# A mixture of experts handing over to a second network: tap weights, row transposes, last copies and half of a weight split put in another order

## The chip, the core and the metric

One core of a Trainium2 chip runs the whole program. TensorE (PE) multiplies and transposes into PSUM, ScalarE (ACT) and VectorE (DVE) copy, cast and compute, GpSimd (POOL) issues gathers and scatters, SyncE (SP) issues the other transfers. Each engine works through a queue of its own. The metric is the device time of the program in microseconds (us); lower is better.

## The reference, cut to what matters

A windowed attention (not touched) makes `x` of 4 x 544 tokens by 512. Then come two networks:

```python
for b in range(B):                       # mixture of experts, one expert e per token
    for s in range(S):
        h = np.maximum(x[b, s] @ w1[e], 0.0)
        out[b, s] = p[e] * (h @ w2[e])

h = np.maximum(x @ w_in, 0.0)            # second network, on out
for k in range(K):                       # K = 3 taps along the tokens
    conv_out += conv_w[k][None, None, :] * hp[:, k:k + S, :]
gate = 1.0 / (1.0 + np.exp(-conv_out))
return (h * gate @ w_out).astype(np.float32)
```

A token has 512 features, an expert 1024 hidden ones, and so has the second network.

## The kernel before, in words

Every float32 product is made as three TensorE products of a high and a low part: `split_k` (L1043) makes the parts of a weight block (a cast `h`, by default on ScalarE, and a subtraction `l` on VectorE; blocks 1, 3, 5 and 7 of the second network's output weights have the cast on VectorE too).

**Mixture of experts.** Tokens are sorted by expert into slots of 128 rows. A slot is gathered, turned (`turn_x`), multiplied by `w1` (`layer1`), turned (`turn_h`), multiplied by `w2` (`layer2`), copied from PSUM to `ys` by ScalarE and scattered to `y_dram` by GpSimd. `step` runs slots 2 to 19 as a pipeline. While they run, the second network's weights are loaded and converted. `last(21)` handles slots 20 and 21 together: `p` is 20 and `s` is 21. Each part of a slot stands in a run-time branch (`either`): a slot of at most 32 rows takes the short path `few_l1`, `few_turn`, `few_l2`, which uses unsplit weights; then the second network's weights can be split early, under a branch on the same flag (`r`, L1229 to L1232 for the input weights).

**The passage.** In `last` the order, written out by hand, is: slot 21's rows turned; the input weights split; a sigmoid on a scratch column (L1233, it loads the function table that the second network uses); slot 19's second layer (`layer2(p - 1)`), its copy and scatter; the load of the second network's first rows from `y_dram` (`load0`, five transfers); slot 21's `few_l1`; slot 20's turn; slot 21's `few_turn`; the taps' transpose (`conv_w`, L1184 and L1185); a flag that says whether late tokens touch those rows (`late_flag`, L962 to L964); slot 20's second layer; the five row parts scaled by the gate (`scale0`, VectorE); parts 0 and 1 turned and split (`xt0`: four TensorE transposes, a ScalarE cast, a VectorE subtraction); slot 21's `few_l2` with its four copies (L1422) and the scatter; parts 2 to 4 turned. `run` then reads the flag (L1196, L1197), does the rest only if it is set, and splits the eight blocks of the output weights (`split_out`).

**Second network.** It runs over 32 units (batch `b`, feature block `f`). A unit is 24 products (L1589), a relu (L1613), three taps (L1606, L1608), a sigmoid (L1623), a gating product (L1624) and a split (L1636, L1637). In units 0 to 3 ScalarE also scales the next batch's rows (L1545), which SyncE loads from `y_dram` (L1539) once the last scatter has landed. In program order the first L1545 stands between unit 0's taps and unit 1's relu.

Of the kernel before, what the change touches and what calls it, by code (L numbers as in the profile page):

```python
# [8 lines left out]
F32 = mybir.dt.float32  # L9
# [3 lines left out]
AF = mybir.ActivationFunctionType  # L13
# [4 lines left out]
P = 128  # L18
B, H, SL, SG, DH = 4, 8, 512, 32, 64
S = SL + SG  # L20
DM = H * DH
E, FF = 8, 1024
NKC = DM // P
NFC = FF // P
# [27 lines left out]
def build_masks(nc, pool, masks):  # L52
# [16 lines left out]
    for g in range(2):  # L69
        e = nc.gpsimd if g else nc.vector  # L70
        for t in range(3):
            rows = slice(64 * g, 64 * g + 32)
            for slot, o in enumerate(win_order(t)):
                if o in (0, 2):
                    e.tensor_copy(masks[rows, t, 32 * slot:32 * slot + 32], (lo, hi)[o // 2][rows])
            yield
        rows = slice(64 * g + 32, 64 * g + 64)
        for t in range(2):
            for slot, o in enumerate(win_order(2)):
                dst = masks[rows, t, 32 * slot:32 * slot + 32]  # L80
                if o == 2 * t:
                    e.memset(dst, BIG)
                elif o in (0, 2):
                    e.tensor_copy(dst, (lo, hi)[o // 2][rows])
        yield
# [900 lines left out]
NTS = P // TS  # L986
# [8 lines left out]
FILL = {1: 1, 3: 1, 6: 3, 7: 1, 8: 3, 9: 1, 10: 1, 11: 1, 12: 2, 13: 3, 15: 5, 16: 8}  # L995
HALF = 5
K_LAST = 2
N_GLOB = 6
N_GS = 4
N_Y = 24  # L1000
# [8 lines left out]
def conv64(nc, raw, out, m, lim):  # L1009
    hi, lo = raw[:, :, 1], raw[:, :, 0]  # L1010
    v, a, n = nc.vector, out.bitcast(I32), m.shape[0]
    nc.scalar.activation(m, hi.bitcast(F32), AF.Abs)
    nc.scalar.activation(m.bitcast(I32), m, AF.Sign, bias=lim[0:n], scale=-1.0)
    v.tensor_scalar(a, hi, 3, 0x3FFFFFFF, ALU.logical_shift_left, ALU.bitwise_and)
    v.scalar_tensor_tensor(a, hi, -2 ** 30, a, ALU.bitwise_and, ALU.bitwise_or)
    v.scalar_tensor_tensor(a, lo, 29, a, ALU.logical_shift_right, ALU.bitwise_or)
    v.tensor_scalar(lo, lo, 28, 1, ALU.logical_shift_right, ALU.bitwise_and)
    v.tensor_tensor(a, a, m.bitcast(I32), ALU.bitwise_and)  # L1018
    nc.gpsimd.tensor_tensor(a, a, lo, ALU.add)  # L1019
# [33 lines left out]
class Moe:  # L1053
# [133 lines left out]
    def run(self, cw6, cwr, cw, f2):  # L1187
        nc, W, tc = self.nc, self.W, self.tc
        n = NSLOT - 3
        self.f2 = f2  # L1190
        for s in range(NA, n - 2):
            self.step(s)
            if s == NA + 17:
                conv64(nc, cw6, cwr, f2.x_in[4][0:3 * NFC, 0:P], self.lim)
        self.last(n - 1, cwr, cw)
        r = nc.values_load(self.rt.esi[0:1, 4, 1:2], min_val=0, max_val=P + 1)  # L1196
        with tc.If(r != 0):  # L1197
            r = nc.values_load(self.rt.esi[0:1, 4, 0:1], min_val=0, max_val=NB)
            with tc.If(r > n - NA):
                for s in range(n, NSLOT):  # L1200
                    self.slot(s)
            f2.load0()
            for i in range(5):
                f2.scale0(i, self.ps)
                f2.xt0(i, self.ps)
        self.split_out()

    def last(self, s, cwr, cw):
        nc, W, f2, p = self.nc, self.W, self.f2, s - 1
        self.small(s)  # L1210
        self.layer1(p)
        self.fetch(p, 1)
        self.turn_x(s)
        self.resplit(s, 1)
        x, xs, hp = self.xt.pop(s), self.xs.pop(s), self.h_tile()
        hs = self.tp.tile([P, FF], F32, tag="hs", name="hs")
        ht = tuple(self.tp.tile([P, NFC, P], F32R, tag="g" + q, name="g" + q) for q in "hl")
        y = self.ys[s % 2]

        def split(a, b):  # L1220
            for k in range(a, b):
                W.split_k(1, W.f, k, nc.vector)

        def resplit(a, b):
            with self.tc.If(self.chg[s] != 0):
                for k in range(a, b):
                    W.split_k(2, W.s, k, nc.vector)

        r = nc.values_load(self.rt.esi[0:1, 5, s:s + 1], min_val=0, max_val=1,  # L1229
                           engines=[mybir.EngineType.Activation, mybir.EngineType.DVE])  # L1230
        with self.tc.If(r != 0):
            split(0, NKC)  # L1232
        nc.scalar.activation(self.sig, self.sig, AF.Sigmoid)  # L1233
        self.layer2(p - 1)
        self.fetch(p - 1, 2)
        f2.load0()
        with self.tc.If(self.sm[s] != 0):
            self.few_l1(xs, hp, hs)
        self.turn_h(p)
        self.resplit(p, 2)  # L1240
        t = [self.ps.tile([P, 4, P], F32, tag="tr", name="hlp") for _ in range(2)]

        def full1():
            for k in range(K_LAST):
                self.l1_mm(x, W.t[1], hp, k, range(2))
            split(0, K_LAST)

        tq = self.px.tile([P, 4, P], F32, tag="tr", name="hlq")
        self.either(s, lambda: self.few_turn(hs, tq), full1)
        self.conv_w(cwr, cw)  # L1250
        self.rt.late_flag(s + 1, self.px.tile([P, 4, P], F32, tag="tr", name="lf")[0:1, 0, 0:1])
        self.layer2(p)
        self.fetch(p, 2)
        for i in range(5):
            f2.scale0(i, self.ps)
        resplit(0, 4)
        for i in range(2):
            f2.xt0(i, self.px)
        yp = self.y_tile()

        def full2():
            for k in range(K_LAST, NKC - 1):
                self.l1_mm(x, W.t[1], hp, k, range(2))
            for c in range(2):
                self.l1_mm(x, W.t[1], hp, NKC - 1, (c,))
                self.relu_c(hp, hs, c)
            for a in (0, 4):
                for k in range(4):
                    nc.tensor.transpose(t[a // 4][:, k, :], hs[:, P * (a + k):P * (a + k) + P], self.ident)
                nc.scalar.copy(ht[0][:, a:a + 4], t[a // 4])  # L1270
            for a in (0, 4):
                self.lo_t(ht, a, t[a // 4])
            split(K_LAST, NKC)

        self.either(s, lambda: self.few_l2(hs, yp, y), full2)
        resplit(4, NFC)
        with self.tc.If(self.sm[s] == 0):
            for k in range(NFC):
                self.l2_mm(ht, W.t[2], yp, k)
            nc.scalar.copy(y, yp)  # L1280
        self.scatter(s, y)
        for i in range(2, 5):
            f2.xt0(i, self.ps if i == 4 else self.px)

    def split_out(self):
        nc, W = self.nc, self.W
        for k in range(NFC):
            W.split_k(2, W.f, k, nc.gpsimd if k in POOL_F else nc.vector, nc.vector if k in DVE_F else None)

    def slot(self, s):  # L1290
        nc, W = self.nc, self.W
        xs = self.gather(s)
        e = self.reg(nc.sync, 0, s, E - 1)
        for n, w in ((1, self.w1), (2, self.w2)):
            W.load(n, w[bass.ds(e, 1)])
        hs = self.tp.tile([P, FF], F32, tag="hs", name="hs")
        self.turn(xs, NKC)
        hp, yp = self.h_tile(), self.y_tile()
        for k in range(NKC):
            for c in range(2):  # L1300
                nc.tensor.matmul(hp[c], xs[:, P * k:P * k + P], W.s[1][:, k, 512 * c:512 * c + 512],
                                 start=k == 0, stop=k == NKC - 1)
        for c in range(2):
            self.relu_c(hp, hs, c)
        self.turn(hs, NFC)
        for k in range(NFC):
            nc.tensor.matmul(yp, hs[:, P * k:P * k + P], W.s[2][:, k, :], start=k == 0, stop=k == NFC - 1)
        self.out(s, yp)
# [104 lines left out]
    def few_l2(self, hs, yp, y):  # L1413
        n, w = FF // NTS // P, DM // NTS
        for k in range(NFC):
            j, a = divmod(k, n)
            o = P * (n + a) + TS * j
            for i in range(NTS):
                self.nc.tensor.matmul(yp[TS * i:TS * i + TS, 0:w], hs[:, o:o + TS], self.W.s[2][:, k, w * i:w * i + w],
                                      start=k == 0, stop=k == NFC - 1)  # L1420
        for i in range(NTS):
            self.nc.scalar.copy(y[P - TS:P, w * i:w * i + w], yp[TS * i:TS * i + TS, 0:w])  # L1422

# [68 lines left out]
class Ffn2:  # L1492
# [191 lines left out]
    def run(self):  # L1684
# [4 lines left out]
        for n in range(N):  # L1689
            if n < N:  # L1690
# [11 lines left out]
                if n == N_GS:  # L1702
                    x2["g"] = self.scaled(xs.pop("g"), GT)
                if n == N_GLOB:
                    self.glob(x2.pop("g"))
                if b + 1 < B and f == N_GLOB:
                    self.put_glob(b + 1, x[b + 1])
# [197 lines left out]
```

## Time and profile before

| what | value |
|---|---|
| median of 3 runs | 611.85 us (610.93 to 612.66) |
| the profiled execution's own time | 610.53 us |
| its span in the trace | 608.6 us |
| TensorE busy | 570.2 us, 94% |
| VectorE, ScalarE, GpSimd busy | 395.0, 331.4, 171.7 us |

The span is the time in the trace from the first instruction to the last; the 1.9 us between it and the own time lie outside it. Busy shares are over the whole program, and the passage is about 25 us of it (from 380 to 405 us), so the change is read from there.

### The profile page before, as it was taken

To read this page: it belongs to the slowest core of one execution; us is meant where nothing else is said; L and a number is where in the kernel's file an instruction comes from. 1 tells how busy PE (TensorE), PEld (TensorE's weight loads), DVE (VectorE), ACT (ScalarE), POOL (GpSimd) and SP (SyncE) were. 2 spreads that over 40 slices of the span, in tenths; PEclk is the share of its full clock that TensorE was granted. 3 is DMA by queue.
4 is the path that set the end of the run, shared out by engine and by line. 5 is a ranking of instruction groups with operands and counts; after the bars stand their busy time and mean duration, and the time that the engine had idled before them with its cause. 6 is when DMAs were issued, how large, how long until landed. Compare 5 with 4: busy or idle time off the path is not lost. (4 is left out here: it accounts for less than half of the span.)

```text
span 608.6 us, 16465 instructions
## 1 busy us (share of the span) xinstructions
PE 570.2 (94%) x6108; PEld 477.5 (78%) x6108; DVE 395.0 (65%) x821; ACT 331.4 (54%) x657; POOL 171.7 (28%) x226
## 2 busy tenths in 40 slices
PE   8789889879888999999999999889899999999997
PEld 7567667666666888887777788679898998998986
DVE  7877676865983857786487884457963574473330
ACT  5764555556324746865566774447762554463441
POOL 7655740025022332243142330010411403300100
PEclk9998999989899999999999999889999999999999
DMA  9989949656327964597366684321110210000001
GB/s 238 209 196 249 244 114 200 188 194 214 136 71 257 339 203 153 197 355 251 96 246 227 257 298 134 119 82 43 53 36 36 69 36 18 36 5 30 36 36 52
DMA packets 60644, 90.58 MB, mean 149 GB/s; under 512 B 25726, under 2 KB 34198, under 8 KB 60504
## 3 DMA queue, kind: packets, MB, share of 16 engines
q1 hardware_dynamic: 57016, 78.93, 42.5%
q0 software_dynamic: 3520, 10.23, 4.8%
q8 instruction: 65, 1.06, 0.8%
q14 instruction: 43, 0.35, 0.2%
HBM read 125.87 MB, written 15.79 MB: 233 GB/s over the span
## 5 line engine op out<-in xcount | busy, mean ns | idle before, releaser
L1608 DVE SCALAR_TENSOR_TENSOR fc<-f_hp,cw,fc 128x544 f32<-128x544 f32 (+2 forms) x66 | 51.4, 779 | 70.1 <-ACT fc L1606 68.7
L1046 DVE TENSOR_TENSOR wl<-ws,wh 128x512 fp32r<-128x512 f32 (+1 forms) x80 | 65.1, 874 | 16.5 <-ACT wh L1045 13.3
L1045 ACT CAST wh<-ws 128x512 fp32r<-128x512 f32 (+1 forms) x84 | 57.9, 772 | 2.8 <-DMA ws<-in_moe_w_dram 1.8
L1126 PE MATMUL yp<-wh,gh 128*128 128x512 f32 x136 | 55.9, 411 | 1.1 <-ACTq L1340 0.9
L1126 PE MATMUL yp<-wl,gh 128*128 128x512 f32 x136 | 54.8, 403 | 0.4 <-DVEq L1340 0.4
L1666 PE MATMUL f<-wh,fh 128*128 128x512 f32 (+1 forms) x144 | 54.8, 380 | 0.0
L1666 PE MATMUL f<-wh,fl 128*128 128x512 f32 (+1 forms) x144 | 54.4, 378 | 0.0
L1666 PE MATMUL f<-wl,fh 128*128 128x512 f32 (+1 forms) x144 | 54.4, 378 | 0.0
L1126 PE MATMUL yp<-wh,gl 128*128 128x512 f32 x136 | 54.4, 400 | 0.0
L278 ACT ACTIVATE pr<-sp,nm 128x128 f32<-128x128 f32 x128 | 36.6, 376 | 25.0 <-DVE nm L275 25.0
L1083 POOL DMA_INDIRECT y_dram<-ys,sidx x22 | 24.3, 1102 | 90.2 <-ACT ys L1447 30.2
L1110 PE MATMUL hp<-wl,xh 128*128 128x512 f32 x136 | 43.9, 394 | 2.1 <-DVEq L1340 1.1
L1110 PE MATMUL hp<-wh,xh 128*128 128x512 f32 x136 | 45.3, 405 | 0.4 <-PE hlp L1433 0.2
L1071 POOL DMA_INDIRECT xs<-x_dram,gidx x22 | 25.6, 1163 | 70.2 <-ACT pr L278 34.0
L1110 PE MATMUL hp<-wh,xl 128*128 128x512 f32 x136 | 43.6, 392 | 0.0
L1318 ACT ACTIVATE hs<-hp 128x512 f32<-128x512 f32 x34 | 18.7, 596 | 43.1 <-PE hp L1110 42.2
L1613 ACT ACTIVATE f_hp<-f 128x544 f32<-128x544 f32 x31 | 19.4, 624 | 34.7 <-PE f L1589 34.6
L1019 POOL TENSOR_TENSOR wf<-wf,fx 128x512 int32<-128x512 int32 x16 | 20.9, 1308 | 60.0 <-DVE wf L1018 54.7
L1675 ACT COPY fy<-f 128x512 f32<-128x512 f32 (+1 forms) x18 | 10.1, 564 | 46.6 <-PE f L1666 46.6
L1126 PEld LDWEIGHTS yp<-wh,gh 128*128 128x128 f32 x136 | 26.3, 193 | 8.4 <-issue 2.3
L1110 PEld LDWEIGHTS hp<-wl,xh 128*128 128x128 f32 x136 | 25.1, 188 | 9.0 <-DVEq L1340 2.1
L1666 PEld LDWEIGHTS f<-wh,fl 128*128 128x128 f32 x144 | 27.1, 188 | 5.1
(384 smaller groups left out, 1514.2 us busy)
## 6 DMA issues: line engine op xcount, KB each, us to landing
ws<-in_moe_w_dram SPq DMA_DIRECT2D x42, 2048.0 KB
fx<-y_dram SPq DMA_DIRECT2D x17, 256.0 KB
raw<-in_k_l_dram SPq DMA_DIRECT2D x16, 256.0 KB
x_dram<-x SPq DMA_DIRECT2D x16, 256.0 KB
fx<-in_moe_w_in_dram SPq DMA_DIRECT2D x8, 512.0 KB
fx<-in_moe_w_out_dram SPq DMA_DIRECT2D x8, 512.0 KB
out_dram<-fy SPq DMA_DIRECT2D x16, 256.0 KB
VA<-in_v_l_dram SPq DMA_DIRECT2D x20, 192.0 KB
```

Source lines behind the costliest of these rows:

```text
L278: nc.scalar.activation(pr[:, hp, :], sp[:, hp, :], AF.Exp, bias=nm[:, hp:hp + 1], scale=-1.0)
L1019: nc.gpsimd.tensor_tensor(a, a, lo, ALU.add)
L1045: (cp.tensor_copy if cp else self.nc.scalar.copy)(h, src[n][:, k, :])
L1046: eng.tensor_tensor(l, src[n][:, k, :], h.bitcast(F32), ALU.subtract)
L1071: self.nc.gpsimd.indirect_dma_start(out=xs, out_offset=None, in_=self.x_dram[0:n, :], in_offset=bass.IndirectOffsetOnAxis(ap=self.rt.gidx[ ...
L1083: self.nc.gpsimd.indirect_dma_start(out=self.y_dram[:, :], out_offset=bass.IndirectOffsetOnAxis(ap=self.rt.sidx[:, s:s + 1], axis=0), in_= ...
L1110: self.nc.tensor.matmul(hp[c], a[:, k, :], b[:, 512 * c:512 * c + 512], start=k == 0 and m == 0, stop=k == NKC - 1 and m == 2)
L1126: self.nc.tensor.matmul(yp, a[:, k, :], b, start=k == 0 and m == 0, stop=k == NFC - 1 and m == 2)
L1318: self.nc.scalar.activation(hs[:, 512 * c:512 * c + 512], hp[c], AF.Relu)
L1608: nc.vector.scalar_tensor_tensor(c[:, a:b], hp[:, a + t:b + t], self.cw[:, t, f:f + 1], c[:, a:b], ALU.mult, ALU.add)
L1613: self.nc.scalar.activation(hp[:, 1:S + 1].rearrange("p (a c) -> p a c", a=2), p[:, :, 0:272], AF.Relu)
L1666: self.nc.tensor.matmul(yp[:, cs], x[:, c], w[:, cs], start=f == 0 and n == 0, stop=f == NFC - 1 and n == 2)
```

## The change

The taps' transpose moves ahead of the input weights' split, the late flag ahead of `few_l1`, and the table load behind `few_turn`. All five row parts are turned ahead of `few_l2`; slot 21's copies and scatter (`out_last`, `few_y`) move behind the branch on the flag. If slot 21 is short, blocks 0 to 3 of the output weights are split right behind `layer2(p)` in the program, blocks 4 to 7 where all eight were.

```diff
+K_OUT = 4
...
-        self.last(n - 1, cwr, cw)
+        yp = self.last(n - 1, cwr, cw)
         r = nc.values_load(self.rt.esi[0:1, 4, 1:2], min_val=0, max_val=P + 1)
         with tc.If(r != 0):
+            self.out_last(n - 1, yp)
...
-        self.split_out()
+        self.out_last(n - 1, yp)
+        with tc.If(self.few_last != 0) as c:
+            self.split_out(range(K_OUT, NFC))
+        with c.Else():
+            self.split_out()
...
-        r = nc.values_load(self.rt.esi[0:1, 5, s:s + 1], min_val=0, max_val=1,
-                           engines=[mybir.EngineType.Activation, mybir.EngineType.DVE])
+        r = self.few_last = nc.values_load(self.rt.esi[0:1, 5, s:s + 1], min_val=0, max_val=1,
+                                           engines=[mybir.EngineType.Activation, mybir.EngineType.DVE])
+        self.conv_w(cwr, cw)
         with self.tc.If(r != 0):
             split(0, NKC)
-        nc.scalar.activation(self.sig, self.sig, AF.Sigmoid)
         self.layer2(p - 1)
         self.fetch(p - 1, 2)
         f2.load0()
+        self.rt.late_flag(s + 1, self.px.tile([P, 4, P], F32, tag="tr", name="lf")[0:1, 0, 0:1])
         with self.tc.If(self.sm[s] != 0):
             self.few_l1(xs, hp, hs)
...
         self.either(s, lambda: self.few_turn(hs, tq), full1)
-        self.conv_w(cwr, cw)
-        self.rt.late_flag(s + 1, self.px.tile([P, 4, P], F32, tag="tr", name="lf")[0:1, 0, 0:1])
+        nc.scalar.activation(self.sig, self.sig, AF.Sigmoid)
         self.layer2(p)
         self.fetch(p, 2)
+        with self.tc.If(r != 0):
+            self.split_out(range(K_OUT))
         for i in range(5):
             f2.scale0(i, self.ps)
         resplit(0, 4)
-        for i in range(2):
-            f2.xt0(i, self.px)
+        for i in range(5):
+            f2.xt0(i, self.ps if i == 4 else self.px)
         yp = self.y_tile()
...
-        self.either(s, lambda: self.few_l2(hs, yp, y), full2)
+        self.either(s, lambda: self.few_l2(hs, yp, None), full2)
         resplit(4, NFC)
         with self.tc.If(self.sm[s] == 0):
             for k in range(NFC):
                 self.l2_mm(ht, W.t[2], yp, k)
-            nc.scalar.copy(y, yp)
+        return yp
+
+    def out_last(self, s, yp):
+        y = self.ys[s % 2]
+        self.either(s, lambda: self.few_y(yp, y), lambda: self.nc.scalar.copy(y, yp))
         self.scatter(s, y)
-        for i in range(2, 5):
-            f2.xt0(i, self.ps if i == 4 else self.px)
...
-    def split_out(self):
+    def split_out(self, ks=range(NFC)):
         nc, W = self.nc, self.W
-        for k in range(NFC):
+        for k in ks:
             W.split_k(2, W.f, k, nc.gpsimd if k in POOL_F else nc.vector, nc.vector if k in DVE_F else None)
...
-        hp, yp = self.h_tile(), self.y_tile()
+        hp, yp = self.h_tile(), self.px.tile([P, DM], F32, tag="tr", name="yp")
...
+        if y is not None:
+            self.few_y(yp, y)
+
+    def few_y(self, yp, y):
+        w = DM // NTS
         for i in range(NTS):
             self.nc.scalar.copy(y[P - TS:P, w * i:w * i + w], yp[TS * i:TS * i + TS, 0:w])
```

## Rows read from the trace of the kernel before

**Rows 1.** The page's first part: busy time of each engine.

```profile
PE 570.2 (94%) x6108; PEld 477.5 (78%) x6108; DVE 395.0 (65%) x821; ACT 331.4 (54%) x657; POOL 171.7 (28%) x226
```

**Rows 2.** The chain that ended last, in order of time: start, us, what.

```profile
435.33 0.30 POOL fxl L1573
435.68 6.15 PE f L1589 x46
```

**Rows 3.** Windows of 1 us: busy time by engine, granted clock, DMA share, GB/s.

```profile
389.00:390.00 1.00, 0.00 (x0) 0.00 (x0) 0.62 (x2) 0.37 (x1) 0.00 (x0) 1.00 0.69 262
...
392.00:393.00 1.00, 1.00 (x4) 0.81 (x3) 0.00 (x0) 0.00 (x0) 0.00 (x0) 0.50 0.54 139
```

**Rows 4.** Timeline ahead of slot 20's second layer: start, us, engine, line, operation.

```profile
381.51 3.90 ACT L1045 CAST wh<-wf 128x1024 fp32r<-128x1024 f32 x4 [1.16 <-DMA y_dram<-ys,sidx]
385.43 1.28 ACT L1233 ACT_TABLE_LOAD   x1
...
388.33 1.29 DVE L1103 TENSOR_TENSOR gl<-hlp,gh 128x512 fp32r<-128x512 f32 x2 [1.10 <-ACT gh L1434]
...
390.14 0.18 DVE L1185 COPY cw<-cwp 128x24 f32<-128x24 f32 x1 [0.53 <-DVEq L1349]
...
390.38 0.16 PE L962 MATMUL lf<-c_ones,late 128*1 128x1 bf16 x1 [1.88 <-DVE esi L963]
...
391.10 0.40 PE L1126 MATMUL yp<-wl,gh 128*128 128x512 f32 x1
...
391.56 0.56 PE L1126 MATMUL yp<-wh,gh 128*128 128x512 f32 x1
...
394.91 0.46 PE L1126 MATMUL yp<-wh,gl 128*128 128x512 f32 x1
```

**Rows 5.** Timeline from slot 20's second layer to slot 21's copies.

```profile
394.05 0.47 DVE L1513 TENSOR_SCALAR fx<-fx,gate 32x512 f32<-32x512 f32 x1 [3.32 <-DMA fx<-y_dram]
...
397.12 0.49 DVE L1513 TENSOR_SCALAR fx<-fx,gate 128x512 f32<-128x512 f32 x1 [0.53 <-DMA fx<-y_dram]
...
397.74 0.39 PE L1126 MATMUL yp<-wh,gl 128*128 128x512 f32 x1
...
398.22 0.59 ACT L1447 COPY ys<-yp 128x512 f32<-128x512 f32 x1 [8.82 <-PE yp L1126]
...
399.01 2.29 PE L1419 MATMUL yp<-ws,hs 128*32 128x128 f32 x64
...
399.21 0.29 DVE L1523 TENSOR_TENSOR f_x0l<-f_tr,f_x0h 128x128 fp32r<-128x128 f32 x1 [1.60 <-ACT f_x0h L1522]
399.73 0.69 DVE L1523 TENSOR_TENSOR f_x0l<-f_tr,f_x0h 128x512 fp32r<-128x512 f32 x1 [0.23 <-ACT f_x0h L1522]
...
401.44 1.50 PE L1520 MATMUL f_tr<-ident,fx 128*128 128x128 f32 x12
401.46 1.10 ACT L1422 COPY ys<-yp 32x128 f32<-32x128 f32 x4 [1.76 <-PEq L1277]
```

**Rows 6.** Timeline of the output weights' split and the second network's first products.

```profile
404.75 2.18 ACT L1045 CAST wh<-wf 128x512 fp32r<-128x512 f32 x4 [0.28 <-ACTq L1197]
...
405.53 0.59 PE L1589 MATMUL f<-f_x0l,wh 128*128 128x272 f32 x1 [0.56 <-DVEq L1197]
...
405.78 0.69 DVE L1046 TENSOR_TENSOR wl<-wf,wh 128x512 fp32r<-128x512 f32 x1 [0.36 <-DVEq L1197]
...
408.51 1.29 DVE L1046 TENSOR_TENSOR wl<-wf,wh 128x512 fp32r<-128x512 f32 x2
```

**Rows 7.** Timeline of SyncE and ScalarE in the second network's first units.

```profile
406.02 25.21 SPq L1539 DMA_DIRECT2D fx<-y_dram  x8
...
413.35 0.72 ACT L1545 ACTIVATE fx<-fx,gate 128x512 f32<-128x512 f32 x1 [1.81 <-DMA fx<-y_dram]
413.98 0.61 ACT L1613 ACTIVATE f_hp<-f 128x544 f32<-128x544 f32 x1
...
417.87 0.75 ACT L1606 ACTIVATE fc<-f_hp,cw 128x544 f32<-128x544 f32 x1 [0.84 <-DVE fg L1624]
```

More of the change, by code (lines that the diff above doesn't have):

```diff
@@ L1217, in last @@
         ht = tuple(self.tp.tile([P, NFC, P], F32R, tag="g" + q, name="g" + q) for q in "hl")
-        y = self.ys[s % 2]
         def split(a, b):
```

## The prediction, as it was put on record

> **What bounds the kernel now.** I read the busy shares first, then the chain that ended last, then the timeline of the passage engine by engine, because a share over 608.6 us says nothing about 25 of them. TensorE is busy 94% of the span [rows 1], so a delay that TensorE meets is paid in full unless the stretch behind it has slack. The chain shows where slack ends: at 435.68 us unit 8's first products follow at once on GpSimd's copy of 435.33, and from there to the end the chain is mostly TensorE [rows 2]. What matters is what sets 435.68. In units 1 to 7 it is ScalarE, fed by VectorE. At 413.35 ScalarE takes up the first row scaling after waiting 1.81 us for its transfer; unit 1's relu comes right behind at 413.98, and the next gap is a wait for VectorE, 0.84 us before 417.87 [rows 7]. So the path runs: slot 21's last copy of ys, its scatter, the row load, the first L1545, seven units on ScalarE and VectorE, unit 8. The last copy ends at 401.46 + 1.10 = 402.56 [rows 5], and L1545 starts 10.8 us later [rows 7]. I therefore ask one question: when does the last copy end after the change?
>
> All offsets below count from E, the end of slot 20's second layer, 397.74 + 0.39 = 398.13 [rows 5]. The last copy now ends at E + 4.43.
>
> **Up to E: what the moved tap turn, flag and table load give.** TensorE stands idle for 1.88 us before the flag's product at 390.38, which comes just after VectorE's taps copy of 390.14 to 390.32; the second product of slot 20's layer starts at 391.10 [rows 4], and the window from 389 shows no TensorE work [rows 3]. Both small products move to places where VectorE has long answered or nothing behind them needs the answer, and they cost TensorE about the same there. The new limit is VectorE: gl is done at 388.33 + 1.29 = 389.62, and VectorE reaches its next instruction 0.52 us later [rows 4]. I put the second product at 390.2, a gain of 0.9 us. The bounds are 0 (it waits as now) and 1.7 (it follows the turn without waiting, at 389.4). The idle time had a second price: eight products from 391.56 to 394.91 took 3.35 us where the pitch just before was 0.46 / 2 = 0.23 us [rows 4], with a granted clock of 0.50, the lower level, in that stretch [rows 3]. At the higher level they take 1.84, so 1.5 us come back if the remaining gaps leave the clock alone; 0 if not. I take both: 2.4 us, between 0 and 3.2.
>
> The table load, 1.28 us at 385.43 [rows 4], moves behind `few_turn`, where ScalarE next waits 8.82 us for slot 20's products [rows 5]. That wait hides it; uncovered it would cost its 1.28 us. It frees slot 19's copy and scatter by about as much, so the five first loads come earlier too, but they already land before E (the scalings run from 394.05 to 397.12 [rows 5]). They take nothing off the path.
>
> **From E on: the split ahead of the row scalings.** Slot 21 is short: the four early casts of the input weights ran at 381.51 [rows 4] and `few_l2` at 399.01 [rows 5]. So the new branch is taken. In the program, block 0's cast on ScalarE stands behind the copy of slot 20's ys, and that copy waits for slot 20's last product. VectorE's first new instruction is the subtraction that needs this cast, and the five scalings, now done by 397.61 under cover of the products [rows 5], stand behind it. So the blocks are not split beside slot 20's layer but behind it, and they take the scalings with them onto the path. In order:
>
> The copy of ys: starts 0.09 after E and takes 0.59, to 0.68 [rows 5]. Block 0's cast: 2.18 / 4 = 0.55 [rows 6], to about 1.25. VectorE's part of blocks 0 to 3: today the same six instructions run from 405.78 to 408.51 + 0.65 = 409.16 [rows 6], so 3.4, to 4.65. Five scalings: 0.47 + 4 x 0.49 = 2.4 [rows 5], to 7.1. Two branches that VectorE passes, at 0.36 each by the gap before 405.78 [rows 6], to 7.8. Low parts of rows 0 and 1: 0.29 + 0.69 [rows 5], to 8.8. These must finish first because all five parts are now turned ahead of `few_l2` and parts 0 to 3 share two PSUM buffers: part 3's turn waits for part 1's subtraction. Turns of parts 3 and 4: 8 of the 12 transposes that took 1.50 [rows 5], so 1.0, to 9.8. `few_l2`: 2.29 and 0.1 for its branch, to 12.2. Then 0.16 and the four copies, 1.10 [rows 5], to 13.45. Overlapped starts on VectorE could shave 0.45 off, so 13.0 is the lower end.
>
> TensorE is empty for about 5.5 us behind E and then does scattered transposes. The trace has the lower clock after 1.88 us of idling [rows 3, 4], so I expect it here. At the lower level the two turns and `few_l2` could take up to twice their 3.3 us; the surcharge lies between 0 and 3.3. I take 1.0, because part of the transposes runs while TensorE waits for VectorE anyway. That makes E + 14.45 against E + 4.43: 10.0 us later.
>
> What the smaller edits cost: the output weights' second half, split under a further branch, is shorter than what stood there (VectorE's eight blocks ran behind 405.78 [rows 6]), and with the load later still it is done before the first L1545, which hides it. The extra PSUM buffer use in `slot` belongs to slots that run only if the flag is set; the flag was not set here, so it costs nothing.
>
> **The sum.** 10.0 - 2.4 = 7.6 us later for the last copy, so for the scatter, the load and the first L1545, and the units behind it have no slack to give back. The profiled execution took 610.53 us (span 608.6 and 1.9 outside), so it would become 618.1. The shown median is 611.85, 1.3 above it; on that scale the forecast is 619.4. Ends: 13.0 - 4.43 - 3.2 = 5.4 and 13.45 + 3.3 - 4.43 = 12.3, so 617.2 to 624.2.
>
> One rule speaks about the link in the middle. The first load is issued at 406.02 and the second of the five is waited for until 413.35 [rows 7], 7.3 us. The Trainium skill ("DMA: Bandwidth & Descriptors", section on the anatomy of one DMA) gives about 2.0 us plus bytes / 436e3 for a transfer, in its fit for GpSimd's path; that is an estimate of 2.6 us for 256 KB. By it L1545 would be ready 4.7 us sooner and TensorE would set the units' pace, which is the second case below; by the row, the sum above stands.
>
> **The rivals.**
>
> *TensorE sets the pace, not the row load.* Then the shift is that of the stream of products, which now runs from 405.53, E + 7.4 [rows 6]. It would follow `few_l2` and a branch: 12.2 + 1.0 + 0.36 = 13.55. So 6.2 - 2.4 = 3.8 later, 615.6; with the best front gain and no surcharge 12.56 - 7.4 - 3.2 = 2.0, 613.9. For it: TensorE's 94%. Against it: ScalarE's wait at 413.35 and the gapless work behind it [rows 7].
>
> *The split really runs beside slot 20's products.* VectorE is then free at E. Parts 0 and 1 are done as today at 399.73 + 0.69, E + 2.3 [rows 5]; the two turns 1.0, `few_l2` 2.4 and the copies 1.26 follow, to E + 7.0. That is 2.5 later, less 2.4: no change, 612.0. Against it is the order on ScalarE.
>
> *Faster: the same, and TensorE sets the pace.* Its stream then starts after the copies at E + 7.0 instead of 7.4, and the front gain stays: 0.4 + 2.4 = 2.8 sooner, 609.0. The point that decides is one event: whether ScalarE's first cast of an output block starts before slot 20's last product. If it does, the change pays.
>
> **How the numbers follow.** Chances: the forecast 0.74; TensorE's pace 0.13; split hidden, no change, 0.08; faster 0.05. 0.3% of the time, 1.8 us, is about what a measurement of this kernel can tell from no change. So faster 0.05, same 0.08, slower 0.87. The range 614 to 623 takes in the second case down to its lower end and the forecast but for its last 1.2 us, and leaves out the other two.
>
> **What would show it in the changed profile.** VectorE should have an idle stretch under slot 20's second layer, no L1513 there, and then subtractions, scalings and low parts back to back behind it. The four L1422 should end about 14 us after slot 20's last product, the first L1545 about 11 us behind them, and TensorE should idle some 5 us after slot 20 at full clock in the layer itself. The forecast is wrong if L1513 still runs under slot 20's products, if unit 1's relu no longer waits for the row load, or if the front gain is larger than 3.2 us.

## The result, and the profile after

| | before | changed |
|---|---|---|
| median of 4 runs on one chip | 611.39 us (608.71 to 612.66) | 617.99 us (617.38 to 618.4) |
| ratio, 95% interval | | 1.011, 1.0079 to 1.0141 |
| the profiled execution's own time | 610.53 us | 618.4 us |
| its span | 608.6 us | 616.6 us |

The change makes the kernel slower by 6.6 us between the medians and by 7.9 between the profiled executions. The forecast was 7.6 and 619.4. Of the runs of the experiments below, two of e6, one of e8 and one of the kernel before beside e5 to e8 were over 1.5% slower than the fastest of their kernel and are left out of medians and ratios.

The busy shares of the changed kernel hardly differ from before [rows 1]; a share over the span doesn't see a passage of 25 us:

```profile
PE 572.3 (93%) x6108; PEld 479.5 (78%) x6108; DVE 393.1 (64%) x821; ACT 331.9 (54%) x657; POOL 172.4 (28%) x226
```

The chain of the changed kernel says where the time is lost. Unit 8's products again follow GpSimd's copy, 7.93 us later than in [rows 2], about the whole difference of the spans (8.0):

```profile
443.26 0.30 POOL fxl L1587
443.61 6.15 PE f L1603 x46
```

Next the timeline of the changed kernel from slot 20's second layer to unit 1 (rows of several engines, in order of time). The lines that the prediction names have moved: L1461 is now the copy of slot 20's ys, L1436 are slot 21's four copies, L1046 and L1047 the cast and subtraction of a weight block, L1527 the row scalings, L1534 to L1537 the row turns, L1428 `few_l2`, L1603 the second network's products, L1559 its row scaling, L1627 its relu.

```profile
389.04 1.29 DVE L1104 TENSOR_TENSOR gl<-hlp,gh 128x512 fp32r<-128x512 f32 x2 [1.14 <-ACT gh L1448]
...
390.44 0.50 PE L1127 MATMUL yp<-wl,gh 128*128 128x512 f32 x1 [0.29 <-DVEq L1349]
...
395.58 0.39 PE L1127 MATMUL yp<-wh,gl 128*128 128x512 f32 x1
...
396.05 0.59 ACT L1461 COPY ys<-yp 128x512 f32<-128x512 f32 x1 [4.43 <-issue]
396.53 1.14 ACT L1046 CAST wh<-wf 128x512 fp32r<-128x512 f32 x2
...
397.19 0.69 DVE L1047 TENSOR_TENSOR wl<-wf,wh 128x512 fp32r<-128x512 f32 x1 [6.86 <-ACT wh L1046]
...
400.65 2.05 DVE L1527 TENSOR_SCALAR fx<-fx,gate 32x512 f32<-32x512 f32 x5
...
401.18 1.68 PE L1534 MATMUL f_tr<-ident,fx 32*128 32x32 f32 x8 [5.21 <-DVE fx L1527]
...
403.20 3.03 PE L1534 MATMUL f_tr<-ident,fx 128*128 128x128 f32 x12 [0.34 <-DVE f_x0l L1537]
...
403.51 0.69 DVE L1537 TENSOR_TENSOR f_x0l<-f_tr,f_x0h 128x512 fp32r<-128x512 f32 x1 [0.37 <-ACT f_x0h L1536]
...
406.15 3.13 PE L1428 MATMUL yp<-ws,hs 128*32 128x128 f32 x64
...
409.50 1.06 ACT L1436 COPY ys<-yp 32x128 f32<-32x128 f32 x4 [2.65 <-PEq L1284]
...
410.84 0.97 POOL L1084 DMA_INDIRECT y_dram<-ys,sidx  x1 [12.74 <-ACT ys L1436]
...
412.90 0.57 PE L1603 MATMUL f<-f_x0h,wh 128*128 128x272 f32 x1 [3.62 <-PEq L1198]
...
413.37 2.80 SPq L1553 DMA_DIRECT2D fx<-y_dram  x5
...
420.59 0.72 ACT L1559 ACTIVATE fx<-fx,gate 128x512 f32<-128x512 f32 x1 [0.46 <-DMA fx<-y_dram]
...
421.87 0.63 ACT L1627 ACTIVATE f_hp<-f 128x544 f32<-128x544 f32 x1 [0.56 <-PE f L1603]
```

E, the end of slot 20's second layer, is now 395.58 + 0.39 = 395.97. VectorE stands idle for 6.86 us while slot 20's products run, and does its subtractions, the five scalings and the low parts behind E, where ScalarE's cast lets it begin. TensorE waits 5.21 us for them. The last copy ends at 410.56, E + 14.59; before it was E + 4.43 [rows 5].

Windows of 1 us show the clock. The columns are those of [rows 3]; the value behind the five busy times is the granted clock, 1.00 for 2.4 GHz and 0.50 for 1.2 GHz.

```profile
391.00:392.00 1.00, 1.00 (x6) 0.81 (x5) 0.00 (x0) 0.61 (x2) 0.00 (x0) 1.00 0.21 74
...
400.00:401.00 1.00, 0.00 (x0) 0.00 (x0) 0.97 (x3) 0.00 (x0) 0.00 (x0) 0.50 0.00 0
...
407.00:408.00 1.00, 1.00 (x28) 0.92 (x20) 0.57 (x1) 0.00 (x0) 0.00 (x0) 0.50 0.00 0
...
410.00:411.00 1.00, 0.00 (x0) 0.00 (x0) 0.00 (x0) 0.95 (x4) 0.16 (x1) 1.00 0.00 0
...
414.00:415.00 1.00, 1.00 (x6) 1.00 (x6) 0.69 (x1) 0.00 (x0) 0.00 (x0) 0.50 0.11 14
415.00:416.00 1.00, 1.00 (x7) 1.00 (x6) 0.00 (x0) 0.00 (x0) 0.00 (x0) 0.50 0.54 174
416.00:417.00 1.00, 1.00 (x6) 1.00 (x6) 0.00 (x0) 0.00 (x0) 0.00 (x0) 0.50 0.50 166
417.00:418.00 1.00, 1.00 (x6) 1.00 (x5) 0.00 (x0) 0.00 (x0) 0.00 (x0) 0.50 0.98 293
418.00:419.00 1.00, 1.00 (x6) 1.00 (x6) 0.00 (x0) 0.28 (x1) 0.00 (x0) 0.57 1.10 225
419.00:420.00 1.00, 1.00 (x10) 1.00 (x9) 0.00 (x0) 0.97 (x2) 0.00 (x0) 1.00 0.90 260
420.00:421.00 1.00, 1.00 (x10) 1.00 (x9) 0.76 (x1) 0.54 (x2) 0.00 (x0) 1.00 0.37 123
421.00:422.00 1.00, 1.00 (x10) 1.00 (x9) 0.81 (x2) 0.44 (x2) 0.00 (x0) 1.00 0.19 72
```

Slot 20's layer now runs at the upper level throughout; before, part of it ran at the lower one [rows 3]. Behind it the clock falls during the 5.21 us without products and stays low through the row turns and most of `few_l2`. Behind `few_l2` it is at 1.00 again while TensorE waits 3.62 us for the stream's first product; unit 0 then runs at 0.50 until about 418.5.

### The profile page after: what moved, and what is told of

Same layout as the page of the kernel before. It is cut to its first block, busy times and chain, and to the rows that moved or that the text cites. A ratio compares the mean times of both kernels' runs of the same rounds, so it can differ in the third digit from the quotient of the medians.

```text
span 616.6 us, 16483 instructions
## 1 busy us (share of the span) xinstructions
PE 572.3 (93%) x6108; PEld 479.5 (78%) x6108; DVE 393.1 (64%) x821; ACT 331.9 (54%) x657; POOL 172.4 (28%) x226
## 5 line engine op out<-in xcount | busy, mean ns | idle before, releaser
L1047 DVE TENSOR_TENSOR wl<-ws,wh 128x512 fp32r<-128x512 f32 (+1 forms) x80 | 65.1, 874 | 15.3 <-ACT wh L1046 13.1
L1046 ACT CAST wh<-ws 128x512 fp32r<-128x512 f32 (+1 forms) x84 | 58.0, 773 | 2.2 <-DMA ws<-in_moe_w_dram 1.0
L1627 ACT ACTIVATE f_hp<-f 128x544 f32<-128x544 f32 x31 | 19.4, 626 | 39.6 <-PE f L1603 39.6
L1603 PE MATMUL f<-f_x0h,wh 128*128 128x272 f32 x128 | 29.1, 304 | 3.6 <-PEq L1198 3.6
```

The lines of the kernel that those rows point to most:

```text
L1046: (cp.tensor_copy if cp else self.nc.scalar.copy)(h, src[n][:, k, :])
L1047: eng.tensor_tensor(l, src[n][:, k, :], h.bitcast(F32), ALU.subtract)
L1603: self.nc.tensor.matmul(p[:, h, 0:272], a[:, fs], c[:, k, 272 * h:272 * h + 272], start=k == 0 and m == 0, stop=k == NKC - 1 and m == 2)
L1627: self.nc.scalar.activation(hp[:, 1:S + 1].rearrange("p (a c) -> p a c", a=2), p[:, :, 0:272], AF.Relu)
```

## The experiments

What stands ahead of the passage is the same in all kernels but for the taps' turn, yet it took 376.4 to 384.5 us in the profiles, so absolute times are poor for this comparison. I read each trace from one fixed event, A: the start of the early casts of the input weights (381.51 before [rows 4], 381.88 in the changed kernel). From the first product of unit 8 to the end of the span all kernels need 172.9 to 173.6 us. So what a kernel gains or loses in the passage is, to about half a microsecond, in the last column but one. That half is not chance alone: the kernels whose clock falls in units 6 and 7 (e1, e2, e3, e5, e9) need 172.9 to 173.3 from there and the others, but for e11 with 173.2, 173.5 to 173.6. What the low clock takes ahead of unit 8 is thus partly given back behind it. Two executions of one kernel, e2 and e9, differ by 0.6 us at unit 1's relu and at unit 8, so smaller differences there, between single traces, tell little. All offsets are starts or ends of instructions in the timelines, in us.

| kernel | E, from A | last copy's end, from E | unit 1's relu, from A | unit 8, from A | ratio to before, 95% interval |
|---|---|---|---|---|---|
| before | 16.62 | 4.43 | 32.47 | 53.59 | 1 |
| changed | 14.09 | 14.59 | 39.99 | 61.16 | 1.011 (1.0079 to 1.0141) |
| e1 no early split | 14.05 | 7.03 | 33.35 | 56.01 | 1.0051 (1.0028 to 1.0075) |
| e2 front alone | 14.08 | 4.71 | 29.88 | 52.52 | 0.9961 (0.994 to 0.9983) |
| e3 split alone | 16.57 | 11.63 | 40.17 | 62.78 | 1.0152 (1.0127 to 1.0178) |
| e4 copies ahead of the branch | 14.11 | 13.28 | 38.38 | 59.51 | 1.0105 (1.0074 to 1.0136) |
| e5 TensorE kept busy | 14.09 | 12.46 | 37.16 | 61.02 | 1.0124 (1.0072 to 1.0175) |
| e6 split under the products | 14.12 | 7.31 | 33.42 | 54.55 | 1.0049 (1.0013 to 1.0086) |
| e7 front, `few_l2` first | 14.08 | 4.42 | 31.52 | 52.69 | 1.001 (0.9978 to 1.0041) |
| e8 front and fill | 14.09 | 4.70 | 29.97 | 51.12 | 0.9985 (0.9952 to 1.0018) |
| e9 front again | 14.11 | 4.65 | 29.26 | 51.94 | 0.9985 (0.9961 to 1.0009) |
| e10 fill again | 14.05 | 4.67 | 30.02 | 51.15 | 0.9977 (0.9955 to 0.9998) |
| e11 both fills | 14.12 | 12.45 | 38.29 | 59.76 | 1.0056 (1.0027 to 1.0085) |

e1 to e4 ran on one chip, e5 to e8 on a second, e9 to e11 on a third, each beside runs of the kernel before.

**e1, the change without its early split.**

```diff
-        with tc.If(self.few_last != 0) as c:
-            self.split_out(range(K_OUT, NFC))
-        with c.Else():
-            self.split_out()
+        self.split_out()
...
         self.layer2(p)
         self.fetch(p, 2)
-        with self.tc.If(r != 0):
-            self.split_out(range(K_OUT))
```

> The changed kernel with all eight output blocks split where they were before, everything else as changed. Theory (the early split holds VectorE's row scalings behind slot 20's second layer): the scalings run under the products again, slot 21's copies end about 7 us behind slot 20's last product instead of 14.6, and the time falls from about 618.0 to 612, no more than 0.5 us from the kernel before. Rival (five turns ahead of the short second layer, or the copies behind the flag's branch, carry the loss): it stays at 615 or above.

612.89 us (10 runs) beside 609.81. The timeline of e1 has the layer's last product and the four copies:

```profile
398.11 0.39 PE L1127 MATMUL yp<-wh,gl 128*128 128x512 f32 x1
...
404.48 1.05 ACT L1431 COPY ys<-yp 32x128 f32<-32x128 f32 x4 [1.84 <-ACTq L1198]
```

Without the split the last copy ends at E + 7.03, where the prediction's rival had put it for a split that costs nothing. The split is worth 14.59 - 7.03 = 7.56 us of the copies' time. The rest of the order (all five parts ahead of `few_l2`, copies behind the branch) costs 7.03 - 4.43 = 2.60, as much as the front gives, and from A the copies end where they did before (21.08, 21.05). By the rival that would be no change, but the time is 3.1 us above before: unit 1's relu is 0.88 later, since the first row scaling starts 11.64 us behind the last copy instead of 10.8, and 1.5 us more go before unit 8, in the way that e2 shows.

**e2, the front alone; e3, the split alone.** Both are edits of the kernel before. e2:

```diff
+        self.conv_w(cwr, cw)
         with self.tc.If(r != 0):
             split(0, NKC)
-        nc.scalar.activation(self.sig, self.sig, AF.Sigmoid)
...
+        self.rt.late_flag(s + 1, self.px.tile([P, 4, P], F32, tag="tr", name="lf")[0:1, 0, 0:1])
...
-        self.conv_w(cwr, cw)
-        self.rt.late_flag(s + 1, self.px.tile([P, 4, P], F32, tag="tr", name="lf")[0:1, 0, 0:1])
+        nc.scalar.activation(self.sig, self.sig, AF.Sigmoid)
```

> The kernel before with only the three edits ahead of slot 20's second layer: taps' turn, late flag and table load moved. Theory: TensorE's wait of 1.88 us and the stretch at the lower clock go, slot 20's layer ends 2.2 us earlier, and so does everything behind it: about 609.2, 2.2 us faster than before. Rival (the row load hides it, as the first row scaling of the second network waits for a transfer anyway): no change, 611.4.

e3, which keeps the order of rows, copies and taps of the kernel before:

```diff
         self.layer2(p)
         self.fetch(p, 2)
+        with self.tc.If(r != 0):
+            self.split_out(range(K_OUT))
...
-        self.split_out()
+        with tc.If(self.few_last != 0) as c:
+            self.split_out(range(K_OUT, NFC))
+        with c.Else():
+            self.split_out()
```

> The kernel before with only the early split of output blocks 0 to 3 added behind slot 20's second layer. Theory: VectorE takes about 4 us longer to reach the scalings and does them uncovered, the short second layer starts some 6 us later and slot 21's copies end 5.7 to 6.4 us later: about 617.4. Rival (the split is harmless, VectorE has room there): at most 612.

e2: 606.83 us (12 runs); e3: 618.41 us (6 runs); before 609.81. The front moves bring E 2.54 us nearer to A, and unit 1's relu 2.59. But unit 8 is only 1.07 earlier: 1.5 us are given back in units 4 to 7. The row of waits of e2 (total, times, longest, in us) and two of its windows show where:

```profile
PE f_tr L1554 <- DVE fxl L1556: 2.8, 1, 2.8
```

```profile
428.00:429.00 1.00, 0.89 (x5) 0.89 (x5) 1.00 (x3) 0.22 (x1) 0.00 (x0) 0.52 0.75 262
429.00:430.00 1.00, 1.00 (x7) 1.00 (x6) 0.76 (x2) 1.00 (x3) 0.00 (x0) 0.50 0.10 37
```

TensorE, which started earlier, gets further ahead of VectorE, waits 2.8 us for it in unit 6, and comes back at the lower clock. e8 tests this. In e3 the last copies end 7.20 us later than before, where 5.7 to 6.4 was expected; `few_l2` takes 3.64 us there instead of 2.29. The split alone costs 9.19 us at unit 8, more than the whole change (1.5 of them in units 4 to 7, where TensorE waits 2.9 us in e3): so it is the main loss, and the front pays back only a part of it.

**e4, the copies ahead of the flag's branch.**

```diff
-        yp = self.last(n - 1, cwr, cw)
+        self.out_last(n - 1, self.last(n - 1, cwr, cw))
...
-            self.out_last(n - 1, yp)
...
-        self.out_last(n - 1, yp)
```

> The changed kernel with slot 21's copies and scatter ahead of the flag's branch, as before. Theory (a second run-time branch behind the flag's holds TensorE, which starts its stream 2.3 us after the copies end): the stream's first product comes 1.7 to 2.0 us earlier, about 410.9, the row load at most 0.3 us earlier, and the time falls by 0.3 to 0.8 us to about 617.4, because the row load and the stream both limit the first units. Rival (the wait is for the PSUM bank that the copies release): the stream starts no earlier.

615.4 us (6 runs), not to be told from the changed kernel's ratio. Behind the last copy the stream's first product starts 2.15 us later, where it was 412.90 - 410.56 = 2.34: my theory, that the branches behind the copies cost this time, falls. The copies end 1.31 us sooner, mostly because `few_l2` took 1.95 us here, at the upper clock, instead of 3.13. The edit gives no reason for that: it stands behind `few_l2`, and up to there the two programs are the same. So the place of the last copies in the changed kernel varies by over 1 us between executions, with the moment at which the clock comes back. What holds the stream behind the copies was not separated, and the expectation's rival, the PSUM bank, stays untested.

**e5, TensorE kept busy behind slot 20.** 24 added products into a tile that nobody reads:

```diff
         self.layer2(p)
         self.fetch(p, 2)
+        self.warm(24)
```

> The changed kernel with 24 added products right behind slot 20's second layer, into a tile that nobody reads. Theory: in the change TensorE stands idle for 5.2 us behind that layer, its clock falls to the lower level, and the work of parts 3 and 4, the few-row products (3.13 us instead of 2.29) and unit 0 of the stream run at that level. Kept busy, the few-row products take about 2.3 us, the last copies end 1 to 2 us earlier, and the row load alone limits the stream: 1.0 to 1.5 us less than the change. Rival: the lower clock is hidden under VectorE's work and the row load, within 0.3 us of the change.

617.46 us (6 runs) beside 609.47: no gain in time. In the timeline of e5 the added products fill the wait and `few_l2` takes 1.96 us:

```profile
395.75 5.60 PE L1081 MATMUL wm<-wh 128*128 128x512 f32 x24
...
404.72 1.96 PE L1429 MATMUL yp<-ws,hs 128*32 128x128 f32 x64
...
407.31 1.06 ACT L1437 COPY ys<-yp 32x128 f32<-32x128 f32 x4 [1.84 <-ACTq L1198]
```

The last copy ends 2.13 us sooner than in the changed kernel and unit 1's relu starts 2.83 sooner, as the theory has it, or more. But unit 8 is where it was: TensorE waits 2.9 us for VectorE in unit 6, and the clock is at 0.50 when it resumes, as in e2. A window of e5:

```profile
436.00:437.00 1.00, 0.39 (x2) 0.39 (x3) 1.00 (x2) 0.41 (x1) 0.00 (x0) 0.50 0.99 365
```

**e6, the split put under slot 20's products.** The changed kernel with the four blocks issued inside the layer, ahead of its copy:

```diff
-        self.layer2(p)
+        def out_blocks():
+            with self.tc.If(r != 0):
+                self.split_out(range(K_OUT))
+
+        self.layer2(p, out_blocks)
...
-        with self.tc.If(r != 0):
-            self.split_out(range(K_OUT))
...
+    def layer2(self, s, mid=lambda: None):
...
+            mid()
             nc.scalar.copy(y, yp)
```

> The changed kernel with the split of output blocks 0 to 3 issued inside slot 20's second layer, ahead of the copy that waits for its last product. Theory: the early split costs its time because ScalarE's first cast stands behind that copy; issued ahead of it, casts and subtractions run under the layer's products, the five scalings end about 1 us behind the layer's end, and the last copies end 7.0 to 7.5 us behind it: 2.5 to 3.5 us above the kernel before, as without the early split. Rival: an early split on these engines delays the passage wherever it stands, since layer and split share VectorE and ScalarE: 5 us or more above the kernel before.

611.45 us (10 runs) beside 609.47. In the timeline of e6 (E is 390.51) ScalarE's first cast now stands ahead of the copy that waits for the layer's end, and VectorE's part follows it under the products:

```profile
386.04 0.60 ACT L1046 CAST wh<-wf 128x512 fp32r<-128x512 f32 x1
...
386.68 0.69 DVE L1047 TENSOR_TENSOR wl<-wf,wh 128x512 fp32r<-128x512 f32 x1 [1.83 <-ACT wh L1046]
...
390.01 2.06 DVE L1534 TENSOR_SCALAR fx<-fx,gate 32x512 f32<-32x512 f32 x5
...
390.54 0.59 ACT L1468 COPY ys<-yp 128x512 f32<-128x512 f32 x1 [2.66 <-PE yp L1127]
...
396.76 1.06 ACT L1438 COPY ys<-yp 32x128 f32<-32x128 f32 x4 [1.83 <-ACTq L1198]
```

The copies end at E + 7.31: 7.28 of the 7.56 us are gone with no work removed, and the layer itself is no longer (E - A 14.12). This is the event on which the prediction had put the change's sign: if the first cast starts ahead of slot 20's last product, "the change pays". It does not. The kernel isn't faster than before (ratio 1.0049, from 1.0013 up): the order behind E, 2.6 us in e1, takes back what the front gives.

**e7, the front with `few_l2` first.** e2 with slot 21's products, copies and scatter directly behind slot 20's layer, and all five row parts behind them:

```diff
-        for i in range(2):
-            f2.xt0(i, self.px)
...
-        for i in range(2, 5):
+        for i in range(5):
```

> The front part of the change alone (filter taps, late flag, table load), with slot 21's few-row products, copies and scatter directly behind slot 20's layer and all five parts of unit 0 behind them. Theory: the last copies end about 0.7 us earlier than with the front part alone, and the row load behind them too: 0.3 to 0.7 us less than the front part alone, about 3 us below the kernel before. Rival: the parts that are moved behind the copies delay unit 0's first product, and the time is that of the front part alone.

609.99 us (12 runs) beside 609.47, no faster than the kernel before. The copies end 0.29 us sooner than in e2, not 0.7, and the gain doesn't reach the load. The timeline of e7:

```profile
399.67 1.10 ACT L1420 COPY ys<-yp 32x128 f32<-32x128 f32 x4 [2.66 <-PEq L1275]
...
402.21 0.97 POOL L1083 DMA_INDIRECT y_dram<-ys,sidx  x1 [3.10 <-ACT f_x0h L1520]
...
406.08 2.57 SPq L1537 DMA_DIRECT2D fx<-y_dram  x5
```

The scatter starts 1.44 us behind the copies (0.55 in e2), by the profile released by the casts of the row parts, and the load is issued 3.87 us behind the scatter (2.76 in e2). Unit 1's relu is 1.64 later than in e2. Earlier copies are worth nothing if what they release stands behind other work. Which of the moved parts holds the load up was not separated.

**e8 and e10, the front with unit 6's wait filled; e9, the front again.** e8 and e10 are one kernel, and e9 is e2. What e8 adds to e2 is 12 products at unit 6 into a tile that nobody reads:

```diff
+    def keep(self, n):
+        t = self.y_tile()
+        for _ in range(n):
+            self.nc.tensor.matmul(t, self.w1[0][0][:, 0:P], self.w1[0][0][:, 0:512], start=True, stop=True)
...
                     self.glob(x2.pop("g"))
+                    self.keep(12)
```

> The front part of the change alone, with 12 added products at unit 6 of the stream, into a tile that nobody reads. Theory: with the front part alone TensorE waits 2.8 us for VectorE's low part in unit 6, its clock falls to 0.50, and unit 7 gives back 1.5 of the 2.6 us that the front part had gained; with the wait filled the clock stays at 1.00, and the time is 1.5 us below the front part alone, about 3.9 us below the kernel before. Rival: the loss in units 6 and 7 is not the clock's, and the added products change nothing or delay the unit.

> The front part of the change alone once more, on one chip with the next kernel. If the front part gains 2.6 us at the stream's first unit and 1.5 us of it is given back in units 6 and 7, its time is 1 to 3 us below the kernel before, as when it first ran; if that first time was chance, it is within 0.5 us.

> The front part with 12 added products at unit 6, whose result nobody reads, beside the front part alone on the same chip. Theory: unit 8 begins 2.5 us earlier than before, from the same starting point, instead of 1.1 us, and the time is about 1.4 us below the front part alone. Rival: a later stage takes the 1.4 us back, and both kernels have the same time to 0.5 us.

e8: 607.32 us (11 runs) beside 609.47; e9: 609.5 and e10: 608.61 beside 610.06 (12 runs each). In the traces the theory holds twice. From unit 3's relu to unit 8 it is 14.90 and 14.88 us with the products, 16.39 and 16.42 without. The timeline of e10 shows the filled wait, and its window the clock:

```profile
421.47 3.00 PE L1561 MATMUL f<-wh 128*128 128x512 f32 x12
424.61 0.66 PE L1554 MATMUL f_tr<-ident,fx 128*128 128x128 f32 x4
```

```profile
425.00:426.00 1.00, 1.00 (x11) 1.00 (x10) 0.82 (x2) 0.72 (x2) 0.00 (x0) 1.00 0.20 76
```

Unit 8 starts 2.47 and 2.44 us earlier than before, in place of 1.07 and 1.65. The run times bear this out only in direction: e10 is 0.9 us below e9, less than either interval tells. Part of the 1.5 us is lost again: counted from A to the end of the span, e8 is 0.85 us below e2 and e10 0.35 below e9. That the front alone is faster was measured once (0.9961) and not the second time (0.9985, an interval that holds 1).

**e11, the changed kernel with both fills.** The edits of e5 and e8 together.

> The changed kernel with the 24 unused products behind slot 20's second layer and the 12 at unit 6. Theory: the 24 alone brought the last copies 2.1 us and the stream's second activation 2.8 us earlier, and the low clock in unit 7 took all of it back; with both, unit 8 begins 2.5 to 2.8 us earlier than in the change, and the time is about 2.5 us below it. Rival: units 6 and 7 are limited by VectorE, and unit 8 stays where it was.

613.97 us (12 runs) beside 610.06, ratio 1.0056. Unit 8 starts 1.40 us earlier than in the changed kernel, not 2.5 to 2.8. TensorE has no wait left in units 4 to 7, and from unit 3's relu to unit 8 it is 15.22 us against 14.89 in the changed kernel. So the missing part has two pieces. The larger lies ahead: unit 1's relu came 1.70 sooner here and 2.83 in e5, with copies that end at the same offset. The first row scaling starts 11.09 us behind the last copy in e11 and 9.98 in e5, and 1.0 of that 1.1 lies between the first issue of the load and the scaling (7.63 against 6.63); why one execution's transfers took longer is open. The smaller piece, the 0.33 us behind unit 3's relu, is TensorE's own: its products, the 12 unused ones among them, run without a wait from the stream's first at 407.97 to unit 8, and unit 0 ran at the lower clock. In e5 unit 0 ran at the upper one. In both TensorE had just waited 3.0 us behind `few_l2`. The windows, e11 first:

```profile
411.00:412.00 1.00, 1.00 (x7) 1.00 (x6) 0.00 (x0) 0.00 (x0) 0.00 (x0) 0.50 0.30 39
```

```profile
411.00:412.00 1.00, 1.00 (x10) 1.00 (x9) 0.96 (x3) 0.00 (x0) 0.00 (x0) 1.00 0.00 0
```

The time is 3.9 us above the kernel before, where the changed kernel's is 6.6. That is about the forecast 2.5 less, but the two were measured on different chips and their intervals meet, and the trace shows only 1.40; so the time does not confirm the theory.

## Why the prediction was right, point by point

**The question asked.** When does the last copy end? From A it ends at 14.09 + 14.59 = 28.68 instead of 21.05, so 7.63 later; the forecast was 7.6. Unit 8 follows by 7.57. That the path runs through this copy, and that the units behind have no slack for a delay, is right: from unit 3's relu to unit 8 it is 14.9 us before and after. That the number fits to 0.1 us is luck, as the steps below show; in e4, where the same instructions lead up to `few_l2`, the last copy ends only 6.34 later.

**The front.** Forecast 2.4 (0.9 and 1.5), measured 2.53 at E in the changed kernel and 2.54 in e2. Slot 20's second product runs at 390.44, 0.11 behind VectorE's gl (389.04 + 1.29). From A that is 8.56 us, where the forecast's 390.2 is 8.69 and the kernel before has 9.59, so the first term measured 1.03 and the second, the layer at the upper clock, the remaining 1.50. That the whole gain reaches the end of the passage holds for the changed kernel. Where nothing else is late (e2, e9) 0.9 to 1.5 us of it is lost again by unit 8, which the prediction didn't see: before, TensorE's wait in unit 6 had left the clock up. That the first loads land ahead of E is no longer so where the split doesn't hold the scalings: the last two, which wait for them, end 1.28 us behind E in e1 and 0.85 in e2. It costs little: part 1's low part ends at E + 2.32 in e1 and E + 2.29 in e2, and the prediction's rival had 2.3.

**The split's place.** The mechanism is shown from both sides: taken out (e1) the copies come 7.56 us earlier, put ahead of the copy of ys (e6) 7.28. It isn't the work of the four blocks that costs the time, it is where their first cast stands in ScalarE's queue; VectorE's order is the same in e6 as in the change. The prediction's rival went further, to a change that pays once this cast starts early; e1 and e6 show that it doesn't, since the rest of the order costs what the front gives.

**Behind E, step by step.** In the changed kernel: copy of ys to E + 0.67 (forecast 0.68), scalings to 6.73 (7.1), low part of part 1 to 8.23 (8.8), turns of parts 3 and 4 to 10.26 (9.8), `few_l2` to 13.31 (12.2 without the surcharge), copies to 14.59 (13.45, or 14.45 with it). The total hides two errors that cancel. At the upper clock the sum is 1.0 too long: e5, where the added products hold the clock at 1.00 through `few_l2`, ends at 12.46 instead of 13.45, most of it in the low parts (7.74 instead of 8.8) and in `few_l2`, which takes 1.96 instead of 2.29. The 0.7 for two branches on VectorE ahead of the low parts is not to be seen: the first low part starts 0.15 us behind the scalings (402.85 against 400.65 + 2.05). And the surcharge for the lower clock, taken as 1.0, is 14.59 - 12.46 = 2.1 in this execution and 13.28 - 12.46 = 0.8 in e4.

**From the copy to unit 1.** The prediction carried the shift over unchanged. From the last copy's end to the first row scaling it is 10.03 instead of the 10.8 of [rows 7], and then unit 1's relu waits 0.56 for TensorE: both its candidates, the row load and TensorE's pace, end within a microsecond of each other here. One of the prediction's own signs of being wrong, a relu that no longer waits for the row load, is thus half met: the row scaling just ahead of it still waits for its transfer, the relu itself for TensorE. The rival "TensorE sets the pace" was right about this last wait and wrong about the price, since TensorE is itself late: the stream starts 2.3 us behind the copies, where the rival had 0.36 for a branch, and unit 0 runs at the lower clock. e4 shows that moving the copies ahead of the flag's branch does not remove the 2.3; what it is stays open. In e5 and e11 it is 1.3, and there the profile puts the wait down to ScalarE's casts of output blocks, which stand right behind the copies; no run tests this.

**The row load.** The prediction went by the row of 7.3 us against an estimate of 2.6. The changed kernel shows 420.59 - 413.37 = 7.2 for the same load. The Trainium skill ("DMA: Bandwidth & Descriptors", the section on the anatomy of one DMA) prices one transfer alone, and here five of 256 KB are under way together. By the windows, 14 + 174 + 166 + 293 + 225 + 260 + 123 + 72 = 1327 GB/s over windows of 1 us make 1.33 MB from 414 to 422, about the five transfers, and the scaling that needs the second starts at 420.59, when some 90% of that has moved. The same page (section on issuing engines and DMA queues) says that transfers started by ScalarE, SyncE or GpSimd run on the same 16 DMA engines and interleave. All five here are SyncE's, so this trace doesn't test that; it shows that the second of five is usable only when most of all five has moved.

## What to carry to other kernels

Work that is to fill an idle engine must be issued ahead of the instruction that waits for the end of the cover, on every engine that has a part in it: one cast behind a waiting copy moved 3.55 us of VectorE's work (397.19 to 400.74), and what was queued behind it, onto the path. Ask of any reordering what stands in front of its first instruction in each queue, not how idle the engines are. And follow a gain to a point behind which the kernel runs as before (here unit 8): the front's 2.5 us were there at unit 1 and partly gone six units later.

## What the runs showed of the hardware that was not expected

The lower clock can take back a gain. In unit 6 TensorE waited 0.9 (changed kernel, e7), 1.7 (before), 1.9 (e4) and 2.4 us (e6) and kept the granted clock of 1.00. Where it waited 2.2 (e9), 2.8 (e2) and 2.9 us (e1, e3, e5) the clock was at 0.50 when it resumed or, in e9, about a microsecond later, and unit 8 came 1.5 to 2.7 us later, counted from unit 3's relu. The end of the wait in e6 and in e9:

```profile
427.45 0.66 PE L1575 MATMUL f_tr<-ident,fx 128*128 128x128 f32 x4 [2.39 <-DVE fxl L1577]
```

```profile
428.22 0.65 PE L1554 MATMUL f_tr<-ident,fx 128*128 128x128 f32 x4 [2.24 <-DVE fxl L1556]
```

The longer of the two kept the clock and the shorter lost it; behind `few_l2` the same 3.0 us kept it in e5 and lost it in e11; and in slot 20's layer before, 1.88 us of idling was enough [rows 3, 4]. So the length of a gap doesn't decide it, and no run here shows what does. 12 unused products of 0.25 us each in the gap kept the clock up (e8, e10).
